# v loaded in long rows and turned twice by the PE, in a fused attention and spectral-mix kernel

## The chip, the cores and the metric

The kernel runs on one core of a Trainium2 chip. The metric is device microseconds of that core. A core has five engines that run side by side and meet only at semaphores: PE (TensorE: matrix products and transposes into PSUM), DVE (VectorE), ACT (ScalarE), POOL (GpSimd) and SP (SyncE), which here issues the DMAs. Sixteen DMA engines move the data. PE loads one operand as weights (PEld in the profile) and streams the other.

## The reference

Two layers in one kernel. The first is sliding-window attention with a linear bias (B = 8 batches, H = 8 heads, S = 576 positions, D = 64); the second works on its output, read as x of shape (8, 576, 512).

```python
rel = pos[:, None] - pos[None, :]
scores = q @ k.T / sqrt(D)
scores = where((rel >= 0) & (rel < 128), scores - slope[h] * abs(rel), -1e9)
x = softmax(scores) @ v                      # heads side by side: 512 columns
X = rfft(x, axis=1)[:, :64]                  # 64 modes
Y = X @ (w_r[m] + 1j * w_i[m])               # a 512x512 complex matrix per mode
u = x + irfft(Y, n=S, axis=1)
out = u + relu(u @ w_ch)
```

q, k and v are 9.4 MB each, the mode weights w_r and w_i together 134 MB, the output 9.4 MB, all float32.

## The kernel before

**Units and slots.** Attention is cut into 32 units: one batch and one pair of heads (128 of the 512 columns) each. GROUPS splits the four head pairs into group 0 (the first pair; 8 units) and group 1 (the other three; 24 units, the three pairs of a batch in a row). `_slot(g, n, ...)` writes out one step of a software pipeline by hand, and the order in it is the order on every engine: the first half of unit n's scores, PE transposes of q and k of unit n+1, a pair of modes of the spectral layer, the second half of the scores, the casts on POOL for later units, the spectrum of unit n-2, the AV product of unit n-1, the second mask product of unit n.

**One unit.** `_load_unit` loads q and k: a row of 2304 bytes (nine positions of 64) for each of 128 partitions, 64 partitions for each head. POOL casts to bf16 (`_cast_qk`, L400). `_tr` (L423) transposes 64x64 blocks, the two heads on the two diagonal quadrants of the PE array, 18 per tensor. `_evac` (L431) lets ScalarE copy each transposed tensor from PSUM to SBUF. `_score` (L450, L458) computes scores with 64 keys per product, even and odd keys apart, four quadrants of the array at a time. ScalarE takes the exponential (L462), and DVE multiplies by a mask made once per head, which holds the bias and the window (L467, L472). `_av` (L496, L502) multiplies with v and a column of ones, whose sum gives the softmax denominator; DVE divides and writes x (L507 to L513). PSUM has one score tile (`sc`) and two tiles for transposes (`tqk`), used in turn.

**v.** `_load_v` fetches 512 positions of each head with two positions (512 bytes) as the unit of a row, `_load_vt` the last 64 positions of eight batches at once on POOL's DMA queue. POOL casts v into the layout that AV reads (`_cast_v`, L412, four casts per unit; `_cast_vt`, L392).

**The spectral layer.** When the last unit of a batch in a group is done, `_spectrum` (L542) transforms x with a cosine and sine matrix F. Mode weights stream through a ring in SBUF of 12288 float32 per partition: 64 parts of 512 KB for group 0 (32 pairs of modes), 64 parts of 1536 KB for group 1. SP issues a part (`_load_w`, L668) as soon as the products that used its place are through, in one queue with the loads of q, k and v. Group 0's products (`_modes`, L716) are shared out over the slots: four steps a slot, seven in the last ten attention slots and in the slots behind. `_select` (L581 to L590) rearranges the spectrum for the next eight modes, with a DVE cast and a ScalarE copy; it happens eight times for group 0. Group 1's products (`_modes_wide`, L752) come after attention, together with the product with w_ch; each waits for its part. Then `_finish` builds and writes the output.

Of the kernel before, what the change touches and what calls it, by code (L numbers as in the profile page):

```python
# [16 lines left out]
P = 128  # L17
# [6 lines left out]
VB = 6  # L24
QK = 9
# [19 lines left out]
def kernel(  # L45
# [23 lines left out]
    g.units = units = [(j, s, b) for j, grp in enumerate(GROUPS) for b in range(B) for s in grp]  # L69
    N = len(units)  # L70
    g.first = [units.index((j, grp[0], 0)) for j, grp in enumerate(GROUPS)] + [N]
# [12 lines left out]
    g.unit, g.acc = {}, {}  # L84
# [13 lines left out]
    with tc.manual_schedule(engines={ET.SP, ET.PE, ET.Activation, ET.DVE, ET.Pool}):  # L98
        with ExitStack() as wctx:
# [5 lines left out]
            with ExitStack() as actx:  # L105
# [5 lines left out]
                g.mask = cp.tile([P, NP, 2, 512], BF16)  # L111
                g.vbs = [cp.tile([P, 8, 72], BF16, name=f"vb{i}") for i in range(3)]
                g.vbt = cp.tile([P, NP, B, 72], BF16)
                g.qpool = actx.enter_context(tc.tile_pool(name="qk", bufs=QK))
                g.vpool = actx.enter_context(tc.tile_pool(name="v", bufs=VB))
                g.vts = actx.enter_context(tc.tile_pool(name="vts", bufs=2))
# [9 lines left out]
                for n in range(n0):  # L126
                    _load_unit(g, n)
                    if n < VB - 1:
                        _load_v(g, n)
                    elif n >= VB + 2:  # L130
                        _load_v(g, n - 3)
                    if n >= g.first[1] - 1:
                        for _ in range(4 // JOINT[0]):
                            _load_w(g)
                with tc.tile_pool(name="tmpc", bufs=1, side="right") as tp:
                    _consts(g, tp)
                    _cast_qk(g, 0)
                    for s in GROUPS[0]:
                        _load_vt(g, s)
                    _cast_qk(g, 1)  # L140
                    _cast_v(g, 0)
                    for s in GROUPS[0]:
                        _cast_vt(g, s)
                    _tr(g, 0, 0)
                    _tr(g, 0, 1)
                    _evac(g, 0, 0)
                    _evac(g, 0, 1)
                    first = dict.fromkeys(u[1] for u in units[:2])
                    rest = [s for s in range(NP) if s not in first]
                    for s in first:  # L150
                        _mask(g, tp, s)
                    for n in range(3):
                        _slot(g, n, [], [])
                    for s in rest:
                        _mask(g, tp, s)
# [5 lines left out]
                for j in range(len(GROUPS) - 1):  # L161
                    steps = []
                    for n in range(g.first[j + 1] + 2, g.first[j + 2] + 2):
                        steps += [n] * (SHARE if n < N - LA else SHARE_END)
# [7 lines left out]
                for n in range(3, N + 2 + TAIL):  # L172
                    if g.first[1] <= n and loaded < N + 3:
                        if loaded < N:
                            _load_unit(g, loaded)
                        _load_v(g, loaded - 3)
                        loaded += 1
# [68 lines left out]
def _consts(g, tp):  # L246
# [7 lines left out]
    nc.gpsimd.iota(reli, [[1, 256]], base=0, channel_multiplier=-2)  # L254
    rel3i = tp.tile([P, 64], I32)
    nc.gpsimd.iota(rel3i, [[1, 64]], base=0, channel_multiplier=-1)
# [3 lines left out]
    for vb in g.vbs:  # L260
        nc.gpsimd.memset(vb[:, :, g.D : g.D + 1], 1.0)
    nc.gpsimd.memset(g.vbt[:, :, :, g.D : g.D + 1], 1.0)
# [35 lines left out]
    nc.vector.tensor_scalar_add(rel[64:128, 0:256], rel[64:128, 0:256], 127.0)  # L298
    nc.vector.tensor_copy(rel[:, 448:512], rel3i)
    nc.vector.tensor_scalar_add(rel[64:128, 448:512], rel[64:128, 448:512], 64.0)  # L300
# [10 lines left out]
def _mask(g, tp, s):  # L311

    for hh in range(2):
        g.nc.scalar.activation(
            g.mask[:, s, hh], g.rel, AF.Exp, scale=-(2.0 ** (-8.0 * (2 * s + hh + 1) / g.H)))
# [42 lines left out]
def _load_unit(g, n):  # L358
    nc = g.nc
    _, s, b = g.units[n]  # L360
    u = g.unit.setdefault(n, Ctx())
    u.q = g.qpool.tile([P, g.R, g.D], FP32, tag="q", name=f"q{n}")
    u.k = g.qpool.tile([P, g.R, g.D], FP32, tag="k", name=f"k{n}")
    for t, src in ((u.q, g.q), (u.k, g.k)):
        nc.sync.dma_start(
            out=t.rearrange("p r d -> p (r d)"),
            in_=src[b, 2 * s : 2 * s + 2].rearrange("h (p r) d -> (h p) (r d)", r=g.R))


def _load_v(g, n):  # L370

    _, s, b = g.units[n]
    u = g.unit.setdefault(n, Ctx())
    u.v = g.vpool.tile([P, 2, 2, 2, g.D], FP32, tag="v", name=f"v{n}")
    for hh in range(2):
        g.nc.sync.dma_start(
            out=u.v[:, hh].rearrange("p k r d -> p k (r d)"),
            in_=g.v[b, 2 * s + hh, 0:512, :].rearrange("(k p r) d -> p k (r d)", k=2, r=2))


def _load_vt(g, s):

    vt = g.vts.tile([P, g.B, g.D], FP32, tag="vt", name=f"vt{s}")
    for hh in range(2):
        g.nc.gpsimd.dma_start(
            out=vt[64 * hh : 64 * hh + 64],
            in_=g.v[:, 2 * s + hh, 512:576, :].rearrange("b p d -> p b d"))
    g.unit["vt", s] = vt


def _cast_vt(g, s):
    g.nc.gpsimd.tensor_copy(g.vbt[:, s, :, 0 : g.D], g.unit.pop(("vt", s)))  # L392


def _cast_qk(g, n):
    u = g.unit[n]
    u.b = []
    for w, t in enumerate((u.q, u.k)):
        tb = g.work.tile([P, g.R, g.D], BF16, tag=f"qkb{w}", name=f"qkb{w}")
        g.nc.gpsimd.tensor_copy(tb, t)  # L400
        u.b.append(tb)


def _cast_v(g, n):

    u = g.unit[n]
    u.vb = g.vbs[n % 3]
    o = u.vb[:, :, 0 : g.D].rearrange("p (k i h) d -> p i k h d", k=2, i=2)
    v = u.v.rearrange("p h k r d -> p r k h d")
    for r in range(2):  # L410
        for i in range(2):
            g.nc.gpsimd.tensor_copy(  # L412
                o[64 * r : 64 * r + 64, i], v[64 * i : 64 * i + 64, r])


def _tr(g, n, w):

    u = g.unit[n]
    tp = g.ps1.tile([P, g.R, 64], BF16, tag="tqk", name=f"tqk{w}")
    for r in range(g.R):  # L420
        for hh in range(2):
            hs = slice(64 * hh, 64 * hh + 64)
            g.nc.tensor.transpose(  # L423
                tp[hs, r, :], u.b[w][hs, r], g.ident_b[hs, hs], tile_position=(64 * hh, 64 * hh))
    u.tp = getattr(u, "tp", []) + [tp]


def _evac(g, n, w):
    u = g.unit[n]
    dst = g.work.tile([P, g.S], BF16, tag=f"qkT{w}", name=f"qkT{w}")  # L430
    g.nc.scalar.copy(  # L431
        dst.rearrange("c (p r) -> c p r", r=g.R), u.tp[w].rearrange("c r p -> c p r"))
    u.qk = getattr(u, "qk", []) + [dst]


def _score(g, n, w):
# [3 lines left out]
    u = g.unit[n]  # L440
    s = g.units[n][1]
    qT, kT = u.qk
    sc = g.pss.tile([P, 2, 512], FP32, tag="sc", name="sc")
    for i in range(2):
        c = 2 * w + i
        nq = 256 if c < 3 else 192
        for r in range(2):
            for hh in range(2):
                hs = slice(64 * hh, 64 * hh + 64)
                nc.tensor.matmul(  # L450
                    sc[64 * r : 64 * r + 64, hh, 256 * i : 256 * i + nq],
                    lhsT=kT[hs, c * P + r : c * P + P : 2], rhs=qT[hs, c * P : c * P + nq],
                    start=True, stop=True, tile_position=(64 * hh, 64 * r))
    if w:
        for r in range(2):
            for hh in range(2):
                hs = slice(64 * hh, 64 * hh + 64)
                nc.tensor.matmul(  # L458
                    sc[64 * r : 64 * r + 64, hh, 448:512], lhsT=kT[hs, 512:576],
                    rhs=qT[hs, 512:576], start=True, stop=True, tile_position=(64 * hh, 64 * r))  # L460
# [3 lines left out]
    if not w:  # L464
        a = a.rearrange("p h (i q) -> p h i q", i=2)
        m = g.mask[:, s, :, 0:256].unsqueeze(2).broadcast_to([P, 2, 2, 256])
# [3 lines left out]
def _mask3(g, n):  # L470
    a = g.unit[n].att[1]
    g.nc.vector.tensor_tensor(out=a, in0=a, in1=g.mask[:, g.units[n][1]], op=ALU.mult)  # L472


def _av(g, n):
# [6 lines left out]
    po = 64 * (b % 2)  # L482
    ps = slice(po, po + 64)
# [4 lines left out]

    for t in range(ST):
        o, m = (slice(0, P), P) if t < 4 else (ps, 64)  # L490
        kw = {} if t < 4 else dict(tile_position=(0, po))
        terms = ([(t - 1, P)] if t > 0 else []) + ([(t, 0)] if t < 4 else [])
        for hh in range(2):
            for j, (c, q0) in enumerate(terms):
                q0 += 256 * (c % 2)
                nc.tensor.matmul(  # L496
                    av[o, hh, col(t)], lhsT=att[c // 2][:, hh, q0 : q0 + m],
                    rhs=u.vb[:, 2 * c + hh, 0 : D + 1],
                    start=(j == 0), stop=(t < 4 and j == len(terms) - 1), **kw)
    for hh in range(2):  # L500
        hs = slice(64 * hh, 64 * hh + 64)
        nc.tensor.matmul(  # L502
            av[ps, hh, col(4)], lhsT=att[1][hs, hh, 448:512], rhs=g.vbt[hs, s, b, 0 : D + 1],
            start=False, stop=True, tile_position=(64 * hh, po))
# [472 lines left out]
```

## Time and profile before

| | |
|---|---|
| median of 3 runs | 446.31 us (446.1 to 446.61) |
| profiled execution | 445.02 us, span 443.3 us |
| PE, DVE, ACT, POOL busy | 75%, 49%, 44%, 32% of the span |
| HBM read, written | 163.58 MB, 9.44 MB |
| DMA packets | 51554, of these 16384 of 512 bytes |
| granted PE clock | 0.901 |
| first exponential of attention | starts at 12.64 us |
| first wide product of group 1 | starts at 174.44 us |

The page's first part gives busy time of each engine; a busy PE is not PE at its peak, since products are pipelined. The second cuts the span into 40 slices, a digit for a tenth of the slice. A group of instructions is named by its line, engine, operation, output and inputs, with what it waited for at the end. In the timeline a row is one instruction, or some like ones merged, with start and duration in us, and in brackets the idle time before it and what ended that.

### The profile page before, as it was taken

Reading aid. Unit: us, or ns where it says so; the run is one execution under the profiler, and the core shown is the slowest. Engines: PE = TensorE matmul, PEld = TensorE weight load, DVE = VectorE, ACT = ScalarE, POOL = GpSimd, SP = SyncE. Lnnn points to the kernel's source line nnn. Section 1 sums busy time; section 2 is a strip of 40 time slices with the busy share of each in tenths; the row PEclk is TensorE's granted clock in tenths of the full one; section 3 lists DMA queues with packets and bytes.
Section 4 is the critical chain, followed back from the end, with each engine's and each line's share of the span. In section 5 each row is a group of like instructions: output and inputs, shape, how many; then the busy total and the mean of one; then the engine's idle time right before and its main releaser. Section 6 shows DMA issues by size and latency. Waiting matters only on the chain.

```text
span 443.3 us, 10956 instructions
## 1 busy us (share of the span) xinstructions
PE 331.5 (75%) x4531; PEld 195.0 (44%) x4547; DVE 215.7 (49%) x434; ACT 194.0 (44%) x309; POOL 141.1 (32%) x258
## 2 busy tenths in 40 slices
PE   2577978786888886454476987967878679897993
PEld 2455667675676763111122332322323224464661
DVE  8468567656665661010012544534535345562882
ACT  3787758675765831000011342323323323351794
POOL 6799989887775502020000000000000000000800
PEclk9979669886788875989968999999999998999998
DMA  8999999999999999999999999999999999997598
GB/s 253 357 360 316 388 314 381 387 373 397 393 373 394 416 417 432 421 435 429 430 429 429 430 429 429 427 431 430 430 426 430 430 428 429 427 427 292 202 351 303
DMA packets 51554, 173.73 MB, mean 392 GB/s; under 512 B 4912, under 2 KB 21296, under 8 KB 43440
## 3 DMA queue, kind: packets, MB, share of 16 engines
q1 hardware_dynamic: 51120, 171.99, 97.8%
q0 software_dynamic: 384, 1.05, 1.0%
q8 instruction: 35, 0.57, 0.5%
q14 instruction: 15, 0.12, 0.1%
HBM read 163.58 MB, written 9.44 MB: 390 GB/s over the span
## 4 chain that ended last, share of the span: by engine, by line
DMA 41%; PE 31%; ACT 11%; DVE 8%; issue 4%; POOL 3%; ACTq 0%; POOLq 0%; DVEq 0%; SPq 0%
DMA ring<-in_moe_w_i_dram 26%; DMA ring<-in_moe_w_r_dram 14%; PE acc L752 7%; ACT att L462 6%; PE sc L450 4%; PE xt L542 3%; PE u L882 3%; ACT qkT L431 3%; PE av L496 3%; PE xw L815 2%; PE u L802 2%; POOL vb L412 2%; PE acc L716 1%; POOL qkb L400 1%; PE tqk L423 1%
## 5 line engine op out<-in xcount | busy, mean ns | idle before, releaser
L752 PE MATMUL acc<-ring,Xz 128*32 128x512 bf16 x336 | 90.3, 406 | 51.9 <-DMA ring<-in_moe_w_r_dram 25.6
L820 ACT CAST hl<-xw 64x512 bf16<-64x512 f32 x72 | 41.8, 580 | 93.4 <-PE xw L815 66.0
L462 ACT ACTIVATE att<-sc 128x1024 bf16<-128x1024 f32 x64 | 65.6, 1025 | 29.0 <-PE sc L450 24.1
L752 PEld LDWEIGHTS <-Xz 128*32 128x32 bf16 x336 | 30.6, 97 | 106.3 <-issue 70.3
L821 DVE TENSOR_TENSOR hl<-xw,hl 64x512 bf16<-64x512 f32 x72 | 49.6, 689 | 56.6 <-ACT hl L820 56.6
L412 POOL CAST vb<-v 64x256 bf16<-64x256 f32 x128 | 64.6, 504 | 17.1 <-PE av L496 11.8
L840 POOL MEMSET ZTa<- 32x512 bf16 x2 | 1.0, 516 | 187.8 <-ACT ZTa L838 187.8
L450 PE MATMUL sc<-qkT,qkT 64*64 64x256 bf16 (+1 forms) x512 | 31.8, 325 | 27.9 <-ACT qkT L431 16.3
L431 ACT COPY qkT<-tqk 128x576 bf16<-128x576 bf16 x64 | 40.6, 637 | 0.8 <-PE tqk L423 0.8
L815 PE MATMUL xw<-wch,xT 128*128 128x512 bf16 x139 | 37.1, 386 | 0.8
L423 PE MATMUL tqk<-ident_b,qkb 64*64 64x64 bf16 x1152 | 30.9, 213 | 6.9 <-POOL qkb L400 6.5
L423 PEld LDWEIGHTS <-qkb 64*64 64x64 bf16 x1152 | 30.3, 129 | 9.0 <-POOL qkb L400 8.4
L467 DVE TENSOR_TENSOR att<-att,mask 128x1024 bf16<-128x1024 bf16 x32 | 26.8, 836 | 14.1 <-ACT att L462 13.9
L590 ACT ACTIVATE Xz<-xz 128x192 bf16<-128x192 f32 (+1 forms) x24 | 7.5, 313 | 56.6 <-DVE Xz L587 55.4
L496 PE MATMUL av<-vb,att 128*128 128x65 bf16 (+1 forms) x512 | 31.1, 216 | 1.1 <-DVE att L472 0.9
L400 POOL CAST qkb<-q 128x576 bf16<-128x576 f32 x32 | 27.2, 850 | 5.6 <-PE tqk L423 2.9
L795 DVE COPY xT<-tp 128x512 bf16<-128x512 bf16 x36 | 15.2, 423 | 27.9 <-PE tp L793 27.2
L716 PE MATMUL acc<-Xz,ring 128*128 128x32 bf16 x704 | 25.3, 181 | 4.5 <-DMA ring<-in_moe_w_i_dram 1.8
L496 PEld LDWEIGHTS <-att 128*128 128x128 bf16 (+1 forms) x512 | 24.7, 113 | 7.1 <-DVE att L472 1.4
L450 PEld LDWEIGHTS <-qkT 64*64 64x64 bf16 x512 | 13.3, 119 | 32.9 <-ACT qkT L431 18.8
L400 POOL CAST qkb<-k 128x576 bf16<-128x576 f32 x32 | 26.9, 839 | 0.3 <-DMA k<-in_k_dram 0.2
L716 PEld LDWEIGHTS <-ring 128*128 128x128 bf16 x704 | 21.3, 99 | 10.0 <-DMA ring<-in_moe_w_r_dram 3.6
(111 smaller groups left out, 434.3 us busy)
## 6 DMA issues: line engine op xcount, KB each, us to landing
ring<-in_moe_w_r_dram SPq DMA_DIRECT2D x32, 1536.0 KB, 13.0
ring<-in_moe_w_i_dram SPq DMA_DIRECT2D x31, 1536.0 KB, 13.0
ring<-in_moe_w_i_dram SPq DMA_DIRECT2D x33, 512.0 KB, 7.5
ring<-in_moe_w_r_dram SPq DMA_DIRECT2D x32, 512.0 KB, 6.9
q<-in_q_dram SPq DMA_DIRECT2D x32, 288.0 KB, 6.7
k<-in_k_dram SPq DMA_DIRECT2D x32, 288.0 KB, 6.2
v<-in_v_dram SPq DMA_DIRECT2D x64, 128.0 KB, 5.8
out_dram<-o SPq DMA_DIRECT2D x32, 256.0 KB, 3.4
```

The source lines that it names most:

```text
L400: g.nc.gpsimd.tensor_copy(tb, t)
L412: g.nc.gpsimd.tensor_copy(o[64 * r : 64 * r + 64, i], v[64 * i : 64 * i + 64, r])
L423: g.nc.tensor.transpose(tp[hs, r, :], u.b[w][hs, r], g.ident_b[hs, hs], tile_position=(64 * hh, 64 * hh))
L431: g.nc.scalar.copy(dst.rearrange("c (p r) -> c p r", r=g.R), u.tp[w].rearrange("c r p -> c p r"))
L450: nc.tensor.matmul(sc[64 * r : 64 * r + 64, hh, 256 * i : 256 * i + nq], lhsT=kT[hs, c * P + r : c * P + P : 2], rhs=qT[hs, c * P : c * P ...
L462: nc.scalar.activation(a, sc, AF.Exp, scale=1.0 / math.sqrt(g.D))
L496: nc.tensor.matmul(av[o, hh, col(t)], lhsT=att[c // 2][:, hh, q0 : q0 + m], rhs=u.vb[:, 2 * c + hh, 0 : D + 1], start=(j == 0), stop=(t < ...
L716: nc.tensor.matmul(acc[:, et, :, m0 - c0 : m0 - c0 + n, :], lhsT=wt[:, a, et * P : (et + 1) * P], rhs=X[:, a, m0 % MB // n, 1 - w : 3 - w] ...
L752: nc.tensor.matmul(acc[o], lhsT=X[:, a, i // n, 1 - w : 3 - w].rearrange("p i m b -> p (i m b)"), rhs=wt[:, a], start=(w == 0 and a == 0), ...
L815: nc.tensor.matmul(xw, lhsT=xT[:, dt], rhs=g.wch[:, dt], start=(dt == 0 and n in RELU), stop=(dt == 3))
L820: nc.scalar.copy(g.hl[own, n, h], xw[own])
L821: nc.vector.tensor_tensor(out=g.hl[other, n, h], in0=xw[own], in1=g.hl[own, n, h], op=ALU.subtract)
```

## The change

A unit becomes one head of two batches, and two units in a row (two heads, two batches) form a pair that is loaded and transposed together. q, k and v are all loaded the same way: for a pair, two DMAs of 288 KB per tensor, rows of 2304 bytes, all on SP's queue. POOL casts each tensor of a pair in one instruction. The PE transposes full 128x128 blocks (the columns of two batches side by side), nine per tensor and pair, in two parts of five and four; ScalarE copies each part. The transposed v is turned back by five more 128x128 transposes per unit, in blocks of 128 keys (`_keys`), and DVE copies these into the layout that AV reads. Scores have 128 keys per product, with the two batches on the upper and lower half of the array's rows. Both batches of a unit share a mask, so that it is read by broadcast. The transposes for the next pair are spread over the two slots of a pair: the even slot has q and the first part of v, the odd one k and the second part. The last 64 queries are multiplied with the last 128 keys; x4's two halves are divided apart. The spectra of the two batches come in two slots that follow each other. The loads run four pairs ahead (nine and six units before), and mode products begin one slot later.

The core of the diff:

```diff
-VB = 6
-QK = 9
+QK = 4
+CUT = 5
-    g.units = units = [(j, s, b) for j, grp in enumerate(GROUPS) for b in range(B) for s in grp]
+    g.units = units = [(j, 2 * s + i, b) for j, grp in enumerate(GROUPS) for b in range(0, B, 2)
+                         for s in grp for i in range(2)]
...
+def _load_unit(g, n):
+    _, h, b = g.units[n]
+    h -= n % 2
...
+    for w in (1, 2) if n % 2 else (0,):
+        t = g.qpool.tile([P, 2, g.R, g.D], FP32, tag="qkv"[w], name=f"{'qkv'[w]}{n // 2}")
+        for i in range(2):
+            g.nc.sync.dma_start(
+                out=t[:, i].rearrange("p r d -> p (r d)"),
+                in_=(g.q, g.k, g.v)[w][b + i, h : h + 2].rearrange(
+                    "h (p r) d -> (h p) (r d)", r=g.R))
+        u.raw.append(t)
+def _cast(g, m, w):
+    u = g.pair[m]
+    t = g.work.tile([P, g.R, 2, g.D], BF16, tag=f"qkb{w}", bufs=1, name=f"qkb{w}")
+    g.nc.gpsimd.tensor_copy(t.rearrange("p r b d -> p b r d"), u.raw[w])
...
+def _tr(g, m, w, i):
+    u = g.pair[m]
+    u.tp = tp = g.ps1.tile([P, CUT, P], BF16, tag="tqk", name=f"tqk{w}")
+    for r in range(CUT * i, g.R if i else CUT):
+        g.nc.tensor.transpose(
+            tp[:, r - CUT * i], u.b[w][:, r].rearrange("p b d -> p (b d)"), g.ident_b)
+def _evac(g, m, w, i):
...
+    g.nc.scalar.copy(
+        u.qk[w].rearrange("c h (p r) -> c h p r", r=g.R)[:, :, :, r0:r1],
+        u.tp[:, 0 : r1 - r0].rearrange("c r (h p) -> c h p r", h=2))
+def _keys(g, n):
+    nc = g.nc
+    vT = g.pair[n // 2].qk[2][:, n % 2]
+    tp = g.ps1.tile([P, CUT, P], BF16, tag="tqk", name="tv")
+    for c in range(g.ST):
+        o = min(c * P, g.S - P)
+        nc.tensor.transpose(tp[:, c], vT[:, o : o + P], g.ident_b)
+    g.unit[n].vb = vb = g.vbs[n % 3]
+    nc.vector.tensor_copy(
+        vb[:, :, :, 0 : g.D], tp.rearrange("p c (b d) -> p c b d", b=2))
 def _score(g, n, w):
...
+    parts = ((0, 0, 256), (P, 256, 256)) if w == 0 else ((2 * P, 0, 256), (3 * P, 256, 192), (None, 448, 64))
+    for k0, o, nq in parts:
+        q0 = 4 * P if k0 is None else k0
+        k0 = g.S - P if k0 is None else k0
         for i in range(2):
+            hs = slice(64 * i, 64 * i + 64)
+            nc.tensor.matmul(
+                sc[:, i, o : o + nq], lhsT=kT[hs, k0 : k0 + P], rhs=qT[hs, q0 : q0 + nq],
+                start=True, stop=True, tile_position=(64 * i, 0))
...
 def _slot(g, n, w0, w1):
-    if n == g.first[1] + 2:
-        _select(g, 0, 0)
     if n < N:
         _score(g, n, 0)
-    if n + 1 < N:
-        _tr(g, n + 1, 0)
-        _evac(g, n + 1, 0)
-        _tr(g, n + 1, 1)
+    nxt = (n // 2 + 1, n % 2)
+    if nxt[0] < N // 2:
+        _tr(g, *nxt, 0)
+        _evac(g, *nxt, 0)
+        _tr(g, *nxt, 1)
...
     for w in w0:
         _pair_of_modes(g, *w)
     if n < N:
         _score(g, n, 1)
-    if n + 1 < N:
-        _evac(g, n + 1, 1)
-    if n + 2 < N:
-        _cast_qk(g, n + 2)
-    if n + 1 < N:
-        _cast_v(g, n + 1)
...
+    if nxt[0] < N // 2:
+        _evac(g, *nxt, 1)
+        _tr(g, nxt[0], 2, n % 2)
+        _evac(g, nxt[0], 2, n % 2)
+    if n // 2 + 1 + n % 2 < N // 2:
+        _cast(g, n // 2 + 1 + n % 2, 1 - n % 2)
+        if n % 2:
+            _cast(g, n // 2 + 2, 2)
     if 0 <= n - 2 < N - 1:
-        _spectrum(g, n - 2)
+        _spectrum(g, n - 2, (0,))
+    if 0 <= n - 3 < N - 1:
+        _spectrum(g, n - 3, (1,))
+    if n == g.first[1] + 2:
+        _select(g, 0, 0)
+    if n < N:
+        _keys(g, n)
     if 0 <= n - 1 < N:
         _av(g, n - 1)
```

## The prediction

> **What bounds the kernel now.** I read the page's slices first, then the stretches, then the timeline of one attention slot, then the seam between attention and the long stream of mode weights.
>
> Slices of 11.08 us: granted clock, busy share of the transfers, their rate:
>
> ```profile
> PEclk9979669886788875989968999999999998999998
> DMA  8999999999999999999999999999999999997598
> GB/s 253 357 360 316 388 314 381 387 373 397 393 373 394 416 417 432 421 435 429 430 429 429 430 429 429 427 431 430 430 426 430 430 428 429 427 427 292 202 351 303
> ```
>
> The DMA engines are busy everywhere, yet the first 13 slices move 314 to 397 GB/s and the rest some 430. The cause shows where few weights are loaded (first row, 48 to 66 us, q, k and v only but for its ends) against the pure weight stream:
>
> ```profile
> 48.00:66.00 18.00, 15.32 (x346) 12.13 (x338) 12.00 (x30) 12.56 (x18) 16.03 (x29) 0.72 1.01 344
> ...
> 300.00:390.00 90.00, 72.89 (x473) 30.79 (x480) 42.79 (x75) 28.26 (x52) 1.03 (x2) 0.98 1.01 430
> ```
>
> (last three columns: granted clock, DMA share, GB/s). v comes in 16384 packets of 512 bytes. v is about 30% of the qkv bytes; if the 2304-byte rows run at 400, 344 overall puts v at 1/(1/344 - 0.7/400)*0.3 = some 260 GB/s: 8.4 MB in 32 us, where 400 would take 21. So about 11 us of transfer time is there to be saved.
>
> But is attention paced by transfers? One plain slot (a unit without a spectrum):
>
> ```profile
> 118.37 0.41 PE L450 MATMUL sc<-qkT,qkT 64*64 64x256 bf16 x8 [0.90 <-ACT qkT L431]
> ...
> 118.61 0.74 PE L423 MATMUL tqk<-ident_b,qkb 64*64 64x64 bf16 x36
> 118.84 1.02 ACT L462 ACTIVATE att<-sc 128x1024 bf16<-128x1024 f32 x1 [0.52 <-PE sc L450]
> ...
> 119.28 0.57 PE L716 MATMUL acc<-Xz,ring 128*128 128x32 bf16 x16
> 119.76 0.63 ACT L431 COPY qkT<-tqk 128x576 bf16<-128x576 bf16 x1
> ...
> 119.91 0.39 PE L450 MATMUL sc<-qkT,qkT 64*64 64x256 bf16 x8
> ...
> 120.26 0.78 PE L496 MATMUL av<-vb,att 128*128 128x65 bf16 x16
> 120.38 1.02 ACT L462 ACTIVATE att<-sc 128x1024 bf16<-128x1024 f32 x1
> ...
> 121.30 0.63 ACT L431 COPY qkT<-tqk 128x576 bf16<-128x576 bf16 x1
> ...
> 121.98 0.41 PE L450 MATMUL sc<-qkT,qkT 64*64 64x256 bf16 x8 [0.80 <-ACT qkT L431]
> ```
>
> ScalarE hardly stops: exponential, copy, exponential, copy, each started 0.92, 0.62, 0.92 after the one before; then PE's scores wait for the second copy, and the next exponential starts 0.47 after them, at 122.45. That is a loop of 3.61 us with no DMA in it; the AV product (0.78) runs beside the exponential. Between 20 and 150 us the only wait for a transfer, on any engine that computes, is 1.0 us on POOL. Attention is paced by its own loop, and the mode weights of group 0 are handed to the ring at that pace.
>
> The seam, on PE:
>
> ```profile
> 166.72 1.25 PE L716 MATMUL acc<-Xz,ring 128*128 128x32 bf16 x40
> 168.28 0.39 PE L716 MATMUL acc<-Xz,ring 128*128 128x32 bf16 x8 [0.31 <-DMA ring<-in_moe_w_i_dram]
> 169.50 0.40 PE L716 MATMUL acc<-Xz,ring 128*128 128x32 bf16 x8 [0.83 <-DMA ring<-in_moe_w_r_dram]
> 170.72 0.40 PE L716 MATMUL acc<-Xz,ring 128*128 128x32 bf16 x8 [0.82 <-DMA ring<-in_moe_w_i_dram]
> ...
> 174.44 2.72 PE L752 MATMUL acc<-ring,Xz 128*32 128x512 bf16 x6 [2.04 <-DMA ring<-in_moe_w_r_dram]
> ```
>
> Transfers are late here by only some 4 us of waits. From 174.4 on, 64 parts of 1536 KB follow at 430 GB/s (3.66 us each) and PE waits for each. So the end moves one for one with the moment when the first group-1 part lands; the ring gives it room only when 27 of the 32 pairs of group-0 modes are used up, in slot 32, which began at 159.8.
>
> **The change, part by part**, against the profiled time of 445.02 (span 443.3 and 1.7 around it; the median of the runs, 446.31, lies 1.3 higher).
>
> *v's loads.* 64 DMAs of 512-byte packets and 8 on POOL's queue go; 32 of 288 KB come. Worth up to the 11 us above if transfers paced attention; they do not, so I book none. What hides it: the loop.
>
> *POOL.* Per two units, four casts of 0.85 and eight of 0.50 become three of 1152 columns (twice 0.66 to 1.1 each): 7.4 us become 4 to 6.6. POOL stalled PE by about 1.5 us around 43 to 48 us (PE waited 1.31 and 0.60 for qkb): -1.5.
>
> *PE transposes.* 36 quadrant transposes per unit (0.67 from start to the next kind) become 9 full ones for q or k, 4.5 for v and 5 that turn v back. A full one costs 0.06:
>
> ```profile
> 300.68 0.40 PE L793 MATMUL tp<-ident_b,x_sb 128*128 128x128 bf16 x4
> 300.92 0.38 PE L813 MATMUL xw<-x_sb,ident_b 128*128 128x512 bf16 x1
> ```
>
> (four in 0.24.) So 0.54 + 0.27 + 0.30 for 0.67: +0.44 of PE work.
>
> *Scores.* 20 products on quadrants become 10 on half-arrays with the same columns in each half. The trace has no 64-row by 128-column pair. If the two halves run together, as the quadrants do (8 products of 256 in 0.41), no cost; if not, four of 0.11 in a row instead of two rounds, +0.2 on each score, +0.4 per slot, 13 us in all. I take no cost, since the quadrants are the nearest row, and keep 13 for the range.
>
> *ScalarE's copies.* Two copies of 576 columns become three per slot: 640, 512, and 640 or 512. By 0.59 for 512 and 1.025 for 1024 columns, 640 costs 0.69.
>
> *The new wait.* The five transposes of `_keys` write the buffer that held the second half of q or k. So in the changed order they wait for the copy that ScalarE does after the second exponential, and AV and the next unit's scores stand behind them on PE. The loop becomes: exponential 0.92, copy of 640 0.68, exponential 0.92, copy of 512 0.64, keys 0.30, AV 0.71 (18 products, start to start), scores to exponential 0.47: 4.64 instead of 3.61, +1.03. The third copy (0.64) and the DVE copy of the turned keys (0.53, scaled from 0.42 for 512 columns at L795) lie beside keys and AV. DVE gains also two small x4 products and one reciprocal, about 0.4; with some 3.8 busy of 4.64 it stays off the loop in plain slots.
>
> *Spectrum slots.* There PE is the loop: 152.51 to 156.68, 4.17, at full clock, 5.6 on average. The 1.51 of the spectrum now stands ahead of the keys and covers the new wait; PE's added work stays, +0.5.
>
> *Sum.*
> - Start: pair 0's six copies of q, k and v (0.69 or 0.59 each) follow the sine (ends 7.2), then 1.28 of table load and two masks (1.15): first exponential at 13.6, was 12.64: +1.0.
> - Group 0, 8 slots: 12.64 to 48.45 was 35.8; 8 x 4.64 plus 2.4 for six masks is 39.5: +3.7.
> - Group 1, 24 slots, was 112.1: 17 plain ones at 4.29 and 7 with a spectrum. 17 x 1.03 = 17.5; six spectrum slots +3.0; one fewer of these -0.3: +20.2.
> - Clock: AV took 0.71 at full clock and 1.14 at 83.3 us; keys scale alike. Both are now in the loop: +0.6 in about a quarter of 30 slots, +4.6.
> - Seven selects: their DVE cast stands behind masks that now come later (after a later AV); ScalarE waited about 1.4 for it, I add 0.45 each: +3.
> - POOL -1.5.
>
> That is +31.0: slot 32 begins at 190.8. By then transfers are well ahead (62 MB need 155 us even at 400), so the ring is full and DMA idles. The first group-1 part is issued after one pair, the last unit's AV (which waits about 2.2 for its mask) and a second pair, 3.3 later, and lands 3.7 + 2 after that: 199.8 against 174.4, **+25.4**. The 4 us of lateness at the seam, and the 8.8 between slot 32 and the parts, is what the faster loads do give back. 446.3 + 25.4 = **471.7 us**; I say 471.
>
> **Rivals.**
> - *Transfers pace attention after all* (the other side). For: the DMA share is full and rates are low exactly there. Against: 3.61 without a DMA wait. If so, the first part lands 11 us earlier: 435. It decides where a slot can be kept below about 3.9 us; the new order would have to leave AV outside the loop. 6%.
> - *Nothing measurable*: a loop of some 4.0 us in which the saved 8.8 us at the seam pay for it: 446. 2%.
> - *A colder PE.* Waits of about 1.5 us in each plain slot may keep the clock low throughout: keys 0.48, AV 1.14, scores to exponential 0.77, loop 5.55, 0.91 more in most of 30 slots, less the 4.6 booked: up to 22 more, some 490. For: clock 0.72 from 48 to 66 us. Against: full clock in slots that also waited 0.8 to 0.9. 15%.
> - *The forecast*, 455 to 485: 77%.
>
> The Trainium skill ("TensorE: Matmul & The Clock Gate", Part 1) says that the clock halves after an idle window of about 3.4 us and is released by sustained activity. By that rule waits of 1.5 us alone would not trip it, but a low busy share over a window might; the trace's 0.72 beside a busy PE shows that it is not idleness alone. The skill's "DMA: Bandwidth & Descriptors" (Specifications) puts line rate at 512 bytes and above; by that v's rows would gain nothing. The trace disagrees: 344 against 430 GB/s.
>
> **Range.** Low: without clock, select and scores terms and with a loop 0.25 shorter (8 us), 453; high: the cold clock or serial half-arrays, 490. A change under 0.2% could not be told from none. Faster 6%, same 2%, slower 92%.
>
> **What would show it.** PE idle ahead of the keys' transposes, released by ScalarE's qkT copy, about 1.5 us in plain slots, some 30 us in all; exponentials of successive plain units 4.6 to 5.2 apart; gaps in the DMA share from slice 6 to 16; no wait for the ring in the last group-0 modes; PE's first wide product near 200 us; v's packets of 2304 bytes and an early rate near 400. Wrong would be: AV running beside the second exponential, slots under 4 us, or the end not following the first wide product.

## The result, and the profile after

The changed kernel takes **481.21 us** (median of 4 runs, 479.24 to 481.54); the kernel before, run beside it, takes 446.46 us (446.1 to 447.8). The ratio is 1.0763, 95% interval 1.0727 to 1.08. The forecast was 471 us with a range of 453 to 490. The profiled execution after took 481.54 us with a span of 479.8, so 36.5 us more span than before; 34.75 us is the difference of the medians. In experiments 2 and 8 below, one run of four took over 1.5% longer than the fastest; the ratios leave it out, and the trace there is of that run.

The page's slices of the changed kernel, now 12.0 us each (granted clock, busy share of the transfers, their rate):

```profile
PEclk9969979777997787579899799998999999999798
DMA  8999928998995869999999999999999999997398
GB/s 312 401 410 408 390 88 283 326 344 293 337 333 204 300 229 330 322 353 429 429 426 431 432 430 425 431 430 428 430 427 431 429 428 428 431 428 295 139 342 311
```

Slices 2 to 5 run near 400 GB/s, where the kernel before had 316 to 388. Then the rate breaks down (88 in slice 6, where the ring is full and no mode product has yet emptied it) and stays between 204 and 353 up to slice 18. In six of these 13 slices the DMA share is below 0.9: there at least the transfers wait for attention. The stretch of 40 us from 8 to 48 us, and one that will matter later (columns: window, length, busy time and instructions of PE, PE's weight load, DVE, ACT, POOL; granted clock, DMA share, GB/s):

```profile
8.00:48.00 40.00, 27.10 (x323) 20.39 (x322) 25.68 (x60) 34.28 (x48) 16.20 (x14) 0.87 1.04 405
...
193.00:205.00 12.00, 10.11 (x169) 7.56 (x170) 5.38 (x16) 0.89 (x3) 0.00 (x0) 0.50 0.83 297
```

The same 8 to 48 us in the kernel before moved 341 GB/s at a DMA share of 1.06. So the new loads do what they are meant for, 64 GB/s more over 40 us, 2.6 MB or some 6 us of transfer at 405; the end comes some 35 us later all the same.

Where the time goes is seen in the waits from 20 to 190 us (us in all, times, longest):

```profile
PE tv L395 <- ACT qkT L382: 31.2, 24, 3.2
...
ACT Xz L548 <- DVE Xz L545: 12.5, 7, 3.4
```

PE stands 31.2 us in all ahead of the keys' transposes (`tv`, the five that turn v back), 1.3 us each time, for ScalarE's copy. The second row is the wait of ScalarE's copy in the select for DVE's cast there; it was 9.8 us in seven before and has grown by 2.7. One slot of the timeline:

```profile
45.52 1.02 ACT L419 ACTIVATE att<-sc 128x1024 bf16<-128x1024 f32 x1 [0.87 <-PE sc L415]
...
47.06 1.04 ACT L419 ACTIVATE att<-sc 128x1024 bf16<-128x1024 f32 x1
...
47.97 1.37 ACT L382 COPY qkT<-tqk 128x512 bf16<-128x512 bf16 x2
...
48.77 0.44 PE L395 MATMUL tv<-ident_b,qkT 128*128 128x128 bf16 x5 [0.70 <-ACT qkT L382]
...
49.04 0.78 PE L454 MATMUL av<-vb,att 128*128 128x65 bf16 x18
...
49.75 0.39 PE L415 MATMUL sc<-qkT,qkT 64*128 64x256 bf16 x4
...
50.19 1.02 ACT L419 ACTIVATE att<-sc 128x1024 bf16<-128x1024 f32 x1 [0.84 <-PE sc L415]
```

Second exponential at 47.06, second copy behind it at 47.97, keys when that copy has left the buffer at 48.77, then AV, the next scores at 49.75, the next exponential at 50.19. One after the other: 4.67 us from first exponential to first exponential, and 4.65 in the slot after.

The seam, PE and SP in one timeline:

```profile
196.89 0.54 SPq L626 DMA_DIRECT2D ring<-in_moe_w_r_dram  x1
...
197.80 0.61 PE L500 MATMUL xt<-F,x_sb 128*128 128x128 bf16 x4 [0.73 <-DVE x_sb L463]
...
203.04 1.89 PE L674 MATMUL acc<-Xz,ring 128*128 128x32 bf16 x64
203.69 0.54 SPq L626 DMA_DIRECT2D ring<-in_moe_w_i_dram  x1
...
206.38 1.52 PE L710 MATMUL acc<-ring,Xz 128*32 128x512 bf16 x6 [0.15 <-DVE Xz L545]
...
212.21 2.72 PE L710 MATMUL acc<-ring,Xz 128*32 128x512 bf16 x6 [4.30 <-DMA ring<-in_moe_w_i_dram]
```

The last group-0 modes run without a wait for the ring: their weights have long been there. But SP issues the first group-1 part at 196.89 and the second only at 203.69, after the last unit's two spectra (197.80 to 203.1; the kernel before had one there, 164.44 to 166.8, since its units span one batch) and a further step of modes. The first wide product comes at 206.38 (before: 174.44); what it waits for last is DVE's cast in the select, not its part. The second waits 4.30 us for its part and comes at 212.21 (before: 178.01, so +34.2). From there the stream runs as before, and the last mode product stands at 442.49 against 408.85, +33.6.

### The profile page after: what moved, and what is told of

Same layout as the page of the kernel before. It is cut to its first block, busy times and chain, and to the rows that moved or that the text cites. A ratio compares the mean times of both kernels' runs of the same rounds, so it can differ in the third digit from the quotient of the medians.

```text
span 479.8 us, 9053 instructions
## 1 busy us (share of the span) xinstructions
PE 349.6 (73%) x3651; PEld 202.0 (42%) x3667; DVE 242.1 (50%) x529; ACT 219.6 (46%) x341; POOL 72.8 (15%) x101
## 4 chain that ended last, share of the span: by engine, by line
DMA 40%; PE 34%; ACT 12%; DVE 9%; issue 3%; SPq 0%; POOL 0%; ACTq 0%; DVEq 0%; POOLq 0%
DMA ring<-in_moe_w_r_dram 28%; DMA ring<-in_moe_w_i_dram 10%; PE acc L710 5%; ACT att L419 5%; ACT qkT L382 5%; PE av L454 5%; PE sc L415 4%; PE u L840 4%; PE tv L395 3%; PE tqk L370 3%; PE xt L500 2%; DVE att L430 2%; DVE x_sb L463 2%; PE acc L674 2%; PE u L760 2%
## 5 line engine op out<-in xcount | busy, mean ns | idle before, releaser
L382 ACT COPY qkT<-tqk 128x640 bf16<-128x640 bf16 (+1 forms) x96 | 67.0, 750 | 0.4 <-PE tqk L370 0.4
L370 PE MATMUL tqk<-ident_b,qkb 128*128 128x128 bf16 x432 | 44.3, 257 | 10.3 <-POOL qkb L360 6.2
L370 PEld LDWEIGHTS <-qkb 128*128 128x128 bf16 x432 | 33.5, 115 | 23.3 <-issue 11.7
L395 PE MATMUL tv<-ident_b,qkT 128*128 128x128 bf16 x160 | 16.6, 245 | 32.2 <-ACT qkT L382 32.2
L415 PE MATMUL sc<-qkT,qkT 64*128 64x256 bf16 (+2 forms) x320 | 31.0, 298 | 11.8 <-ACT att L419 11.6
L360 POOL CAST qkb<-v 128x1152 bf16<-128x1152 f32 x16 | 19.4, 1213 | 95.9 <-PE tqk L370 85.8
L397 DVE COPY vb<-tv 128x640 bf16<-128x640 bf16 x32 | 15.7, 491 | 35.4 <-PE tv L395 35.0
L395 PEld LDWEIGHTS <-qkT 128*128 128x128 bf16 x160 | 12.9, 109 | 35.4 <-issue 34.3
L454 PEld LDWEIGHTS <-att 128*128 128x128 bf16 (+1 forms) x576 | 26.0, 112 | 2.9 <-DVE x L467 0.5
L430 DVE TENSOR_TENSOR att<-att,mask 128x1024 bf16<-128x1024 bf16 x32 | 26.6, 830 | 1.0
L424 DVE TENSOR_TENSOR att<-att,mask 128x1024 bf16<-128x1024 bf16 x32 | 23.8, 744 | 5.4 <-ACT att L419 5.4
```

The source lines that it names most:

```text
L370: g.nc.tensor.transpose(tp[:, r - CUT * i], u.b[w][:, r].rearrange("p b d -> p (b d)"), g.ident_b)
L382: g.nc.scalar.copy(u.qk[w].rearrange("c h (p r) -> c h p r", r=g.R)[:, :, :, r0:r1], u.tp[:, 0 : r1 - r0].rearrange("c r (h p) -> c h p r" ...
L395: nc.tensor.transpose(tp[:, c], vT[:, o : o + P], g.ident_b)
L415: nc.tensor.matmul(sc[:, i, o : o + nq], lhsT=kT[hs, k0 : k0 + P], rhs=qT[hs, q0 : q0 + nq], start=True, stop=True, tile_position=(64 * i, 0))
L430: g.nc.vector.tensor_tensor(out=a, in0=a, in1=m, op=ALU.mult)
L454: nc.tensor.matmul(av[o, i, col(t)], lhsT=a[:, q0 : q0 + m], rhs=u.vb[:, c, i, 0 : D + 1], start=(j == 0), stop=(j == len(terms) - 1), **kw)
```

## The experiments

Theory: the order inside a slot is the cause; keys and AV stand behind ScalarE's second copy, which stands behind the second exponential, and transfers are not the bound. Rivals: ScalarE's added copies are the bound as work; the transfers pace attention.

**1. The second copy of q and k ahead of the second exponential.**

```diff
         _tr(g, *nxt, 1)
+        _evac(g, *nxt, 1)
     if n == N + 1:
...
     if nxt[0] < N // 2:
-        _evac(g, *nxt, 1)
         _tr(g, nxt[0], 2, n % 2)
```

> The changed kernel, with ScalarE's second copy of q or k put ahead of the second exponential; nothing else moves, no engine has less to do. Theory (the keys' transposes wait for a copy that stands behind the second exponential, and AV and the next scores queue behind them): keys and AV go beside the second exponential, the loop of a plain slot becomes 0.92 + 0.68 + 0.60 + 1.03 + 0.05 + 0.47 = 3.75 instead of 4.64, in some 26 plain slots: 23 us less, about 458 us. Rival (ScalarE's third copy or PE's added transposes simply are more work): no gain, 480 us.

Measured 451.41 us (448.28 to 453.79), ratio 1.009 (1.0052 to 1.0128) to the kernel before: 30 us of the loss are gone by the place of one instruction, 7 more than expected. Every engine still has the same work, so the first rival, ScalarE's copies as work, falls here. (The granted clock also rose, to 0.93 from 0.86 over 66 to 150 us; what that adds is not shown.) Its timeline:

```profile
43.91 1.04 ACT L419 ACTIVATE att<-sc 128x1024 bf16<-128x1024 f32 x1
...
44.26 0.45 PE L395 MATMUL tv<-ident_b,qkT 128*128 128x128 bf16 x5
...
44.55 0.78 PE L454 MATMUL av<-vb,att 128*128 128x65 bf16 x18
...
44.82 0.79 ACT L382 COPY qkT<-tqk 128x640 bf16<-128x640 bf16 x1
...
45.26 0.39 PE L415 MATMUL sc<-qkT,qkT 64*128 64x256 bf16 x4
...
45.69 1.02 ACT L419 ACTIVATE att<-sc 128x1024 bf16<-128x1024 f32 x1
```

Keys and AV now run beside the second exponential, only v's copy is left between it and the next, and second exponentials follow each other in 3.91 here (43.91, 47.82), plain slots elsewhere in 3.8. The wait of PE's `tv` for ScalarE is gone from the head of the list of waits.

**2. AV ahead of the keys**, the other way to take AV out of the chain, with the copy left where it is:

```diff
-    if n < N:
-        _keys(g, n)
     if 0 <= n - 1 < N:
         _av(g, n - 1)
+    if n < N:
+        _keys(g, n)
```

> The changed kernel, with AV of the unit before put ahead of the keys' transposes on PE. Theory: AV (0.71) leaves the loop, the wait itself stays; plain slots 3.93, 26 x 0.71 = 18 us less, about 463 us, and less gained than by the copy put first (458). Rival (more work): 480 us.

Measured 471.88 us (median of three, 469.47 to 476.49; a fourth took 479.24), ratio 1.0559 (1.0475 to 1.0643): 9 us worse than expected. The waits from 20 to 190 us in the 479.24 us run:

```profile
PE tqk L370 <- DVE vb L397: 16.5, 24, 1.4
PE tv L395 <- ACT qkT L382: 13.6, 16, 1.9
```

The wait for ScalarE has more than halved, and a new one has come. DVE's copy of the turned keys now stands behind the divisions of AV in DVE's queue, and the next slot's transposes need the buffer that it reads. How much the other three runs lost there is not shown.

**3. The same with DVE's copy of the keys issued ahead of the divisions** (the keys' transposes and their copy are called inside `_av`, after its products):

```diff
+    if n + 1 < len(g.units):
+        _keys_copy(g, n + 1, _keys_pe(g, n + 1))
     avv = av[:, :, 0 : ST * (D + 1)].rearrange("p i (t c) -> p i t c", t=ST)
```

> AV ahead of the keys' transposes on PE, as in the run that gained 7 us, and now also DVE's copy of the turned keys ahead of the divisions of that AV. Theory (there the wait had moved: the next slot's second transposes stood 16.5 us in all for a copy that DVE did after the divisions): the 18 us forecast for AV first come, about 463 us. Rival (AV was not in the loop): 474 us as without it.

Measured 468.17 us (466.41 to 468.32), ratio 1.0477 (1.0432 to 1.0521): 3.7 us less than experiment 2, but the intervals overlap, so no gain over it is shown, and 463 is not reached. Its plain slots take 4.05 (first exponentials at 39.14, 43.19), against 3.61 before and 3.8 to 3.9 with the copy first: the keys still wait for ScalarE (14.2 us in 15 waits).

**4. v's copies from PSUM (one of the three in each slot) on DVE**, to ask whether ScalarE's work, not its order, is the bound:

```diff
-    g.nc.scalar.copy(
+    (g.nc.vector.tensor_copy if w == 2 else g.nc.scalar.copy)(
```

> The changed kernel, with v's transposed parts copied out of PSUM by DVE instead of ScalarE: ScalarE has 0.64 us a slot less to do, DVE as much more; the wait of the keys' transposes stays. Theory (the wait): v's copy lies beside keys and AV anyway, so nothing is gained: 479 to 486 us, later if DVE's masks come late. Rival (ScalarE's work is the bound): 32 x 0.64 = 20 us less, 461 us.

Measured 479.48 us (477.85 to 481.95), ratio 1.0717 (1.066 to 1.0774), whose interval overlaps the changed kernel's. Taking v's third of the copies from ScalarE gains nothing that can be told. But one row of its waits from 20 to 190 us shows that the keys now stand just as long for DVE:

```profile
PE tv L395 <- DVE qkT L382: 31.3, 23, 2.1
```

So this run put one wait in the place of another and does not by itself rule out that rival; experiment 1 does.

**5. The kernel before, with v loaded for the first five units only**: what is a faster v worth if it were free?

```diff
+    if n >= VB - 1:
+        u.v = g.vkept[n % (VB - 1)]
+        return
     u.v = g.vpool.tile([P, 2, 2, 2, g.D], FP32, tag="v", name=f"v{n}")
+    g.vkept = getattr(g, "vkept", []) + [u.v]
```

> The kernel before, with v loaded for the first five units only; later units use these five again (27 of 32 units' long loads of v are left out, 7.1 MB in 512-byte packets; wrong values). Theory (attention is paced by its own loop): only the lateness at the seam can be gained, 4 to 9 us: 438 to 443 us. Rival (transfers pace attention): 27 us of transfer time less at 260 GB/s, about 420 us.

Measured 443.85 us (441.71 to 445.9), ratio 0.9932 (0.9906 to 0.9958). Some 7 MB less to move (27 of 32 units' v), and 3 us gained, 0.85 us short of the expected band. From 80 to 150 us the DMA share fell to 0.89 (1.05 in the kernel before), so the transfers then idled, and slot 32 still began at 159.7 (159.8). Attention did not end earlier at all; the gain lies behind it (246.2 us from slot 32 to the last mode product, 249.0 in the kernel before). Transfers alone do not pace attention in the kernel before.

**6. The changed kernel with each load of v cut into five**, rows of at most 512 bytes:

```diff
+            for r0 in range(0, g.R, 2) if w == 2 else (0,):
+                r1 = min(r0 + 2, g.R) if w == 2 else g.R
...
+                    in_=(g.q, g.k, g.v)[w][b + i, h : h + 2].rearrange(
+                        "h (p r) d -> (h p) (r d)", r=g.R)[:, r0 * g.D : r1 * g.D])
```

> The changed kernel, with each load of v cut into five DMAs of at most two positions (512-byte packets again, the last 256): the long rows alone undone. Theory (the changed kernel's attention is paced by its loop, and DMA has gaps): 480 to 484 us, no more than the extra issues cost. Rival (the long rows gave back part of what the loop cost): 11 us of transfer time more, 492 us.

Measured 496.3 us (495.14 to 498.12), ratio 1.1116 (1.1053 to 1.1179): a miss by 12 to 16 us, and 4 us above the rival too. The stretch from 8 to 48 us, and one row of SP's timeline:

```profile
8.00:48.00 40.00, 26.49 (x303) 19.96 (x302) 22.65 (x57) 32.03 (x45) 15.24 (x13) 0.91 0.80 248
```

```profile
35.16 8.98 SPq L352 DMA_DIRECT2D v<-in_v_dram  x10
```

248 GB/s at a DMA share of 0.80: the engines are not full. Ten small DMAs keep SP's queue busy for 4.8 to 9.2 us, where the two large ones in the changed kernel took 0.9 to 1.95, and weights, q and k stand behind them; POOL's casts wait for v, q and k (35.6, 21.3 and 14.3 us). So this run changed more than the length of a row: a DMA is 64 or 32 KB in place of 288, and there are five times as many. The Trainium skill ("DMA: Bandwidth & Descriptors", Rules for kernel authors) says that under 64 KB one pays mostly overhead; the run agrees in direction, but only one piece in five (32 KB) lies under that, and the run cannot separate size, number and rows.

**7. The clean version: v in packets of 768 bytes**, with as many DMAs of the same size (three pieces with a pad between them in the tile):

```diff
+        shape = [P, 2, 3, 3 * g.D + 8] if w == 2 else [P, 2, g.R, g.D]
...
+                    out=t[:, i, :, 0 : 3 * g.D],
+                    in_=src.rearrange("h (p c r) d -> (h p) c (r d)", c=3, r=3))
```

> The changed kernel with v's loads in packets of 768 bytes instead of 2304, by the same number of DMAs of the same size (the tile has a pad of 32 bytes between the pieces). By the theory (transfers do not pace this kernel's attention; the stream of weights has gaps there) nothing comes of it: 479 to 484 us. The rival says that the length of the rows itself is what the run with five DMAs per load paid for: several us more, 488 or above.

Measured 481.94 us (480.9 to 484.26), ratio 1.0807 (1.0778 to 1.0837), overlapping the changed kernel's interval: the rival of 488 falls, for 768 bytes; 512-byte rows in DMAs of the old size were not run. From 8 to 48 us:

```profile
8.00:48.00 40.00, 27.38 (x309) 20.58 (x310) 24.12 (x58) 32.89 (x46) 16.74 (x14) 0.87 1.05 391
```

391 against 405 GB/s: the rows do matter to the rate, by 3%, and not to the end.

**8. The last modes ahead of the last spectra**, for the seam:

```diff
-    if n == N + 1:
-        _spectrum(g, n - 2)
     for w in w0:
...
     for w in w1:
         _pair_of_modes(g, *w)
+    if n == N + 1 + TAIL:
+        _spectrum(g, N - 1)
```

> The changed kernel, with the last unit's two spectra put behind the last eight products of group 0 instead of ahead of six of them. Theory (the second group-1 part was issued 6.8 us late, because its place in the ring came free only after both spectra, at half clock): it is issued near 198 instead of 203.7, about 5 us less, 476 us. Rival (the seam is late for another reason, such as the transfers themselves): 481 us.

Measured 477.08 us (median of three, 476.24 to 479.26; a fourth took 485.04), ratio 1.0695 (1.0634 to 1.0756): 4 us less by the medians, but the intervals overlap, so alone it is not shown. The seam in the 485.04 us run, whose slot 32 began at 198.17:

```profile
201.91 0.54 SPq L626 DMA_DIRECT2D ring<-in_moe_w_r_dram  x1
...
203.38 0.54 SPq L626 DMA_DIRECT2D ring<-in_moe_w_i_dram  x1
...
212.72 2.74 PE L710 MATMUL acc<-ring,Xz 128*32 128x512 bf16 x6 [0.15 <-DVE Xz L545]
```

The second part is now issued 1.5 us after the first, not 6.8: the spectra were what held it. But the first wide product still stands behind them and the select, and comes 14.6 us into slot 32 (13.2 in the changed kernel), the second 17.8 (19.1). From slot 32 to the last mode product it takes 249.6 us, in the changed kernel 249.3, in the kernel before 249.0.

**9. The copy first, the modes first, and group 0's negation in the select on DVE** (a queue that has just made the cast which ScalarE waited for):

```diff
-        nc.scalar.mul(
+        neg = nc.scalar.mul if j else nc.vector.tensor_scalar_mul
+        neg(
             X[:, r, :, 0].rearrange("p c k m b -> p c k (m b)"),
```

> The changed kernel with the second copy ahead of the second exponential (451 us alone), the last spectra behind the last products, and the negation in the selects done by DVE, so that ScalarE's queue has nothing there that waits for DVE's masks (7 waits, 9 us, in the run with the copy first). Theory: 451 - 4 - 9 = 438 us, faster than before, down to where transfers pace it (62 MB at some 400 GB/s end at 157 us, which would give about 435). Rival (the selects' wait only moves to PE or DVE): 447 us.

Measured 441.44 us (440.63 to 443.07), ratio 0.9894 (0.984 to 0.9947): 10 us below experiment 1, 3 us short of the forecast, and 1.1% faster than the kernel before. The select's wait inside attention is gone, and the last group-0 modes wait for the ring again (0.81 to 0.83 us three times, from 164 us on; in the kernel before from 168): transfers set the pace there.

**10. The same two edits in the kernel before**, as a control (lines of 9 without the copy, which has no counterpart there):

> The kernel before with two edits that have nothing to do with v: the last modes ahead of the last spectra, and the negation of group 0's select on VectorE. ScalarE waits about 1.4 us for VectorE in each of eight selects; if those 10 us leave the loop, transfers become late at the seam (they already are by 4 us), and with v in 512-byte rows they cannot be earlier by much: 440 to 444, at or above the version with long rows and the same edits (441.4). The rival, that the new layout gives nothing even with its order mended: as fast as that version or faster, 436 to 440.

Measured 446.52 us (12 runs, 444.45 to 448.89), ratio 1.0 (0.998 to 1.002): nothing at all, 2.5 us above the expected band. The stretch from 80 to 150 us, here and in experiment 9:

```profile
80.00:150.00 70.00, 56.98 (x1480) 46.70 (x1473) 47.94 (x105) 48.30 (x64) 53.52 (x92) 0.88 1.05 386
```

```profile
80.00:150.00 70.00, 62.08 (x1104) 49.59 (x1102) 60.41 (x153) 59.86 (x82) 25.58 (x21) 0.98 1.02 402
```

and one of the last modes of the control on PE:

```profile
167.20 0.40 PE L717 MATMUL acc<-Xz,ring 128*128 128x32 bf16 x8 [0.84 <-DMA ring<-in_moe_w_i_dram]
```

ScalarE's wait of 9.8 us is gone there too, and the time goes into the ring: six waits in a row at the seam (three in the kernel before), POOL's cast waits 5.9 us for v, and the DMA share is full at 386 GB/s. In the kernel before, the transfers were right behind attention; a faster attention runs into them. In experiment 9 it does so only later. Whether the rows or the rest of the new layout give that room is not shown.

**11. Experiment 9 with v in packets of 768 bytes:**

> The fastest version so far (the second copy ahead of the second exponential, the last modes ahead of the last spectra, the negation of group 0's select on VectorE; 441.4 us) with v in packets of 768 bytes. There the transfers are late at the seam, so a lower rate of v's loads should be paid one for one: if 768-byte packets run as far below the full rate as the estimate for 512 bytes did in part (some 300 against 400 GB/s, 8.4 MB in 28 us and not 21), up to 7 us more, some 445 to 449. If the rows do not matter even there: 441 to 442.

Measured 442.08 us (440.4 to 442.99), ratio 0.9906 (0.9885 to 0.9927): not told apart from experiment 9. Its rate from 8 to 48 us is 392 against 405, as in experiment 7, but the ring still fills before the first mode products at 66 us, and the hole of 55 to 78 us takes the difference back (308 GB/s against 287). By 150 us both have moved the same, 383 GB/s from 12 us on. Against the control it shows what the new layout with its order mended is worth as a whole: 442.08 for 446.52. The length of v's packets, 768 or 2304 bytes, makes no difference to that.

**12. Experiment 9 with eight steps of modes in each of the first slots that have them:**

```diff
-                        steps += [n] * (SHARE if n < N - LA else SHARE_END)
+                        steps += [n] * (8 if n < g.first[j + 1] + 7 else SHARE if n < N - LA else SHARE_END)
```

> The fastest version so far with eight steps of modes instead of the usual number in the first slots that have them, so that the ring is emptied earlier and the gap in the transfers between 55 and 78 us (296 and 278 GB/s in two slices) is filled. If the transfers set the end, the gap's 22 us at two thirds of the rate are worth up to 7 us, less what the modes cost the attention loop there (0.6 us per slot, 4 slots): 436 to 439. If the loop sets the end: 441 to 444.

Measured **440.03 us** (438.68 to 441.27), ratio 0.9863 (0.9839 to 0.9886): the fastest version, though its step from experiment 9 is within the intervals; it lies between the forecast and the rival. The hole is not filled (278 GB/s, since the first mode products start at 66.65 as before them at 66.88); from 80 to 150 us the rate is 411 in place of 402.

## Why the prediction was right, and where not

- *The loop.* Forecast 4.64 for a plain slot, by the chain of exponential, copy, exponential, copy, keys, AV, scores; measured 4.67 and 4.65. That this chain is the cause is shown by experiments 1 and 3: with the copy moved the slot falls to 3.8 or 3.9, with AV moved to 4.05. The idle time ahead of the keys was forecast at some 30 us and is 31.2.
- *Start and group 0.* First exponential at 14.01 for 13.6. Eight slots of group 0 took 40.8 us (14.01 to 54.84) for 39.5.
- *Group 1.* 138.7 us (first scores of slot 8 at 54.41 to the modes of slot 32 at 193.15) against a forecast of 138.4, clock, selects and POOL included. Of these only the select's wait can be read alone: +2.7 for +3. The slots of group 1 took 4.66 to 8.44 us, and plain slots, spectra and clock were not told apart in them, so an agreement within 0.3 us is in part luck. With group 0 and the start, slot 32 begins 33.3 us later, forecast 31.0.
- *The scores' half-arrays at no cost.* Four products of 256 columns take 0.39, as eight on quadrants did: right, the 13 us kept for the range were not needed.
- *v's loads at nothing.* Right for this order: they gained 64 GB/s early, and DMA then idled. But the reason in the forecast, one loop which alone paces attention, is half of it. Experiment 5 frees most of v's transfers and attention ends no earlier, as the forecast has it; but experiment 10 frees the selects' waits in the loop and gains nothing either, for the ring is then late. That fits two bounds within a few us of each other in the kernel before. That it takes both to gain more is argued, not shown: experiments 9, 11 and 12 carry the whole new layout, and the kernel before with both edits was not run. The rival on the other side named the condition, AV outside the loop and slots below 3.9. Experiment 1 met it with 3.8 to 3.9 in plain slots, and still ended at 451.41; with the selects' waits and the seam mended together (experiment 9) the gain was 5 us, not 11.
- *The step that failed: the seam gives back 5.6.* The forecast had the first group-1 part issued 3.3 us into slot 32 and landed 5.7 later, the first wide product with it at 9.0 (14.6 in the kernel before), and the end following one for one. The first issue came 3.74 into the slot, as thought. But the first wide product came at 13.2, at 206.38 and not near 200, and waited last for the select: the forecast left out that PE has the last unit's spectra (now two, 5.3 us at a granted clock of 0.50), the last modes of group 0 and the select ahead of it. Nor does the end follow that product. From slot 32 to the last mode product it takes 249.3 us here, 249.0 in the kernel before, and 249.1 to 250.3 in experiments 1, 3, 4 and 6 to 8, though the second part is issued 1.5 to 6.8 us after the first in them. So the end follows slot 32: that came 33.3 us later, the last mode product 33.6, and nothing was given back. Why this stretch takes the same time whatever comes first in it stays open.
- *The rest of the profiled difference.* 2.9 us lie behind the last mode product (37.3 for 34.45), where the first 11 us ran at a granted clock of 0.69 for 1.00. The tails of the other versions with this loop took 34.0 to 35.6 us, so it belongs to that execution and not to the change.
- *The colder PE.* Not seen: 0.86 granted from 66 to 150 us, where the kernel before had 0.82. The time lies between forecast and this rival for other reasons. At the seam the clock was low, but it was there before too: 0.55 from 160 to 167 us.
- *Two figures of the working do not come out.* The 8.8 us "between slot 32 and the parts" stand in no sum; the sum gives back 31.0 less 25.4, 5.6. And the low end, by its own terms (4.6, 3 and 8 off 471), is some 455, not 453. Neither decides anything here.
- *Rows and rate.* Forecast near 400 early, measured 405. The Trainium skill ("DMA: Bandwidth & Descriptors", Specifications) puts line rate at 512 bytes and above. The traces disagree by 3%: 391 GB/s with v in 768-byte packets and 405 in 2304 (experiment 7), 392 and 405 in experiments 11 and 9.

## What to carry to other kernels

A buffer that is shared in turn carries an order: when a new writer joins it, write out which engine must read the buffer first and what stands ahead of that read in that engine's queue; here one copy behind an exponential cost 30 of 35 us. Take one bound away at a time before calling the other one the bound: the kernel before gained 0.7% with most of v's transfers gone and nothing with the selects' waits gone. Where a stream is to catch up at a seam, write out all that its first product needs, not only its transfer, and measure the whole stretch from there to the end: here it took 249 us before and after.

## What the runs showed of the hardware that was not expected

- PE's granted clock was 1.00 from 178 to 184 us of the changed kernel, fell to 0.50 near 184.8 and stayed there until 205.3, while PE was busy 16.8 of the 20 us from 185 to 205; the longest gap ahead of the fall was 2.40 us, from 181.2. The Trainium skill ("TensorE: Matmul & The Clock Gate", Part 1) names an idle window of some 3.4 us as what halves the clock and a busy one of that length as what releases it. The gap here was shorter than that. The release fits: it came 4.5 us after the last gap (which ended at 200.79), and no stretch without a gap before it was longer than 3.7 us (190.93 to 194.6). The low clock cost the spectra at the seam 0.61 us per four products in place of 0.40.
- Ten DMAs of 32 to 64 KB in a row held SP for up to 9.2 us, and the transfers fell to 248 GB/s at a share of 0.80, with the same bytes to move.
- 128x128 transposes in place of quadrants did not keep PE cold: in experiment 9, with 432 of them for q, k and v, the granted clock from 48 to 150 us was 0.97, and 0.83 in experiment 10, which has the quadrants.
